# Block-sparse attention and an ELU feed-forward on one core: p and x turned on TensorE as float32, split into two float16 parts out of PSUM

## The chip, the cores and the metric

The kernel runs on one core of a Trainium2 chip. The metric is the device time of one execution, in microseconds (us); lower is better. Engines are named as the profile names them: PE (TensorE), ACT (ScalarE), DVE (VectorE), POOL (GpSimd), and SP, which issues most transfers.

## What is computed

```
scores = q @ k.T / sqrt(64), masked to -1e9 outside the allowed 32x32 blocks   # 4 batches x 8 heads, 768 x 768
attn   = exp(scores - rowmax);  attn = attn / (rowsum + 1e-9)
x      = (attn @ v) laid out as [3072, 512]
h      = x @ w_in                                   # 512 -> 2048
g      = where(h > 0, h, exp(min(h, 0)) - 1)
out    = (g @ w_out) as float32                     # 2048 -> 512
```

A block row may look at its own block and the two beside it, at the first and the last block, and at three sampled ones; the first and last block rows look at everything. q, k and v are float32. The weights arrive with eight bytes per element, and the kernel itself takes them apart.

## The kernel before, in words

Every operand of a matmul is carried as two float16 parts, a high one and a low one (value minus high part), so that products come out nearly as exact as float32. A float32 tile is split by three steps: a cast to float16 (the high part), a subtraction (the low part), and, where the contraction needs the other layout, a turn of both parts.

The 3072 rows of x are worked on in 24 units of 128 rows. `attention(u, t, via)` records one unit: q is loaded, split and turned (`qT`, and `qS` with its halves swapped); the sampled keys are copied side by side into `kG` by POOL; the matching rows of v are fetched into `VT` by SP transfers out of a DRAM copy (`vd`) and by POOL's indirect transfers. Then, for each of four pairs of heads (`hp`): the scores on PE (tile `s`), the row maximum on DVE (`m`), the exponential on ACT (`e`, float32), the cast (`p`, high part), the subtraction (low part), the turn of both parts (`pT`), and the product with v on PE (`av`, or `w` by its bank). DVE adds up the parts into `x` (code name `x32`), and after four pairs it normalises x; x is split and turned likewise (`xn`, then `xT`). `ffn(U, t)` records the feed-forward of two units (256 rows): 16 times two products `h`, the ELU in three steps on ACT and DVE (`fe`), its split (`g`), and the products `o` that add into two PSUM banks. The 32 pieces of the weights are loaded, taken apart and split by `weights` while the first units run; nearly all of this is over when the first feed-forward ends.

A turn goes one of two ways, which `via` says. By DMA (`DMA_TRANSPOSE`), or on PE with `turn16`: eight 128x128 float16 transposes (four of the high part, four of the low one) into one PSUM bank, and one copy of 1024 columns out of it, on ACT or DVE. Units 0 to 3 turn q, p and x on PE; units 4 to 13 turn the first two of their four p on PE and the rest by DMA; from unit 14 on everything goes by DMA. Unit 8, the one of the first and last block rows (`sp`), has three p per pair.

What is recorded is a `Plan`: each operation has the engines that may do it with a cost for each, a due time (`t`), and the buffers that it reads and writes. `Plan.order` walks through these in a model of the five engines and of the transfers, and writes down one fixed order for each engine; where an operation may run on two engines, it takes the one that ends it sooner. So a change of a few operations changes the order, and the choice of engine, of everything behind it. Buffers rotate: there are two of `e`, two of `p`, four of `pT`, two of `s` (a PSUM bank each), one `av` and two `o`.

The low part of p is put on POOL or DVE, whichever is free (`LO`), the cast on ACT or DVE (`CAST`), the copy out of PSUM on ACT or DVE (`LEAVE`).

Of the kernel before, what the change touches and what calls it, by code (L numbers as in the profile page):

```python
# [8 lines left out]
F32 = mybir.dt.float32  # L9
# [4 lines left out]
ALU = mybir.AluOpType  # L14
# [211 lines left out]
def kernel(  # L226
# [56 lines left out]
    def const(shape, dtype, name):  # L283
        return sb.tile(shape, dtype, tag=name, name=name)
# [4 lines left out]
    def flat(ap):  # L289
        names = "abcd"[: len(ap.shape) - 1]  # L290
        return ap.rearrange(f"p {' '.join(names)} -> p ({' '.join(names)})")
# [3 lines left out]
    def scaled(eng, dst, src, scale=1.0):  # L295
        if eng == "ACT":
            nc.scalar.activation(dst, src, AF.Copy, scale=scale)
        elif scale == 1.0:
            ENG[eng].tensor_copy(dst, src)  # L299
        else:  # L300
            ENG[eng].tensor_scalar(dst, src, scale, None, op0=ALU.mult)
# [11 lines left out]
    wo = [wo_all[:, f] for f in range(NFC)]  # L313
    kT = [const([P, H, S], F16, f"kT{x}") for x in range(2)]
    kG = const([P, rooms["kG"], 2, H, KW], F16, "kG")
    ident = sb.tile([P, P], F32, tag="x32", bufs=rooms["x32"], name="ident")
    nc.gpsimd.memset(ident, 1.0)
    nc.gpsimd.affine_select(
        ident, ident, pattern=[[1, P]], compare_op=ALU.is_equal, fill=0.0, base=0,
# [54 lines left out]
    def turn16(t, src, dst, via, new=(), w=(), name="", bank="s"):  # L374
# [12 lines left out]
        def leave(e):  # L387
# [3 lines left out]
        plan.add(LEAVE, t, leave, r=[pt], new=new, w=w,  # L391
                 margin=ML, port=False, name=name)

    LO = {"DVE": 0.66, "POOL": 1.2}
    CAST = {"ACT": 0.57, "DVE": 0.43}
    LEAVE = {"ACT": 0.98, "DVE": 0.64}
# [259 lines left out]
    def attention(u, t, via):  # L656
# [105 lines left out]
        for hp in range(H // 2):  # L762
# [46 lines left out]
            for c in range(NC):  # L809
                e32, p, pT = buf("e", [P, 2, 256], F32), buf("p", [P, 2, 512], F16), buf("g" if u == 1 else "pT", [P, 8, P], F16)  # L810
                pts.append(pT)

                def exp(e, c=c, e32=e32, m=m, ss=ss):
                    for y in range(2):
                        nc.scalar.activation(  # L815
                            e32.ap[:, y, :], ss[c].ap[:, y, :], AF.Exp, bias=m.ap[:, 6 + y : 7 + y])
                plan.add({"ACT": 0.82}, t + PITCH * hp + 1, exp, r=[ss[c], m], new=[e32], name=f"ex{u}.{hp}")
                plan.add(CAST, t + PITCH * hp + 1, margin=MC, fn=lambda e, e32=e32, p=p: scaled(e, p.ap[:, 0, :], flat(e32.ap)),
                         r=[e32], new=[p], name=f"ph{u}.{hp}")
                plan.add(LO, t + PITCH * hp + 1, margin=MO, fn=lambda e, e32=e32, p=p: ENG[e].tensor_tensor(  # L820
                    p.ap[:, 1, :], flat(e32.ap), p.ap[:, 0, :], op=ALU.subtract), r=[e32, p], w=[p],
                    name=f"pl{u}.{hp}")
                turn16(t + PITCH * hp + TURN, p, lambda pT=pT: pT.ap, "PE" if hp < via[1] else "DMA", new=[pT], name=f"pt{u}.{hp}", bank=bank)
# [19 lines left out]
            def join(e, hp=hp, av=av):  # L843
# [3 lines left out]
            plan.add({"DVE": 0.45}, t + PITCH * hp + TIMES + 1, join, r=[av],  # L847
                     new=[x32] if hp == 0 else [], w=[x32] if hp else [], port=False, name=f"nx{u}.{hp}")

        def norm(e):  # L850
            total, x = x32.ap[:, :, D], x32.ap[:, :, 0:D]
            nc.vector.tensor_scalar(total, total, 1e-9, None, op0=ALU.add)
            nc.vector.reciprocal(total, total)
            nc.vector.tensor_tensor(x, x, total.unsqueeze(2).to_broadcast([P, H, D]), op=ALU.mult)
        plan.add({"DVE": 0.95}, t + PITCH * 3 + TIMES + 1.5, norm, r=[x32], w=[x32], name=f"nx{u}")
        U, a = u // 2, u % 2
        if a == 0:
            xT[U] = buf("xT", [P, 2, NCC, 2 * P], F16)
        xt = xT[U]
        ts_ = slice(a * P, (a + 1) * P)  # L860
        new = [xt] if a == 0 else []
        xn = buf("xn", [P, 2, DM], F16)
        plan.add(CAST, t + PITCH * 3 + TIMES + 2, margin=MC, fn=lambda e: scaled(e, by_head(xn.ap[:, 0]), x32.ap[:, :, 0:D]), r=[x32], new=[xn], name=f"xh{u}")
        plan.add(LO, t + PITCH * 3 + TIMES + 2, margin=MO, fn=lambda e: ENG[e].tensor_tensor(
# [119 lines left out]
```

## Time and profile before

| | us |
|---|---|
| runs timed, median of 3 (lowest, highest) | 768.63 (768.42, 770.69) |
| the profiled execution, first to last instruction | 780.8 |
| its PE / DVE / ACT / POOL busy | 703.2 / 504.7 / 406.1 / 398.8 |
| PE's granted clock, mean over the span | 0.934 of full speed |

The profiled execution is one of its own, 12.2 us longer than the median of the timed runs; the profile gives its time as its span. Durations are read from it, and differences worked out in it are carried over to the median. An engine counts as busy while one of its instructions runs; a wait is put down to the instruction that ended it.

### The profile page before, as it was taken

The page shows a single profiled execution, that of the slowest core. Times are in us where ns is not written, and L with a number is a line of the kernel's source. Part 1 is how long each engine was busy: PE and PEld are TensorE (multiplying, and loading weights), DVE is VectorE, ACT ScalarE, POOL GpSimd, SP SyncE. Part 2 cuts the span into 40 slices and gives each one's busy share as a digit, 9 for nine tenths or more (in the row PEclk, how much of TensorE's full clock was granted, in tenths as well). Part 3 has the DMA queues.
Part 4 walks back from the last instruction along what each step waited for, and adds up shares of the span by engine and source line. Part 5 has one row for each costly group of instructions (what it writes and reads, how often), then busy time and mean ns, then how long its engine had stood idle before and what let it go on. Part 6 is the DMA issues. An engine that isn't in the chain of part 4 may idle for free.

```text
span 780.8 us, 26302 instructions
## 1 busy us (share of the span) xinstructions
PE 703.2 (90%) x11064; PEld 476.2 (61%) x11064; DVE 504.7 (65%) x849; ACT 406.1 (52%) x723; POOL 398.8 (51%) x605
## 2 busy tenths in 40 slices
PE   6445466999999998999999999999999999999997
PEld 3334355666665765666866766657656667676663
DVE  7788778898866772767677665757555546644121
ACT  4597767897753743535575443425414344342221
POOL 2588567677553345554375454645625337443121
PEclk7555569999999999999999999999999999999999
DMA  9899998889749697769947987987349459652101
GB/s 240 263 275 288 261 257 209 215 158 208 154 91 264 187 192 164 161 133 203 221 87 142 171 149 150 183 144 166 76 94 229 69 103 216 141 97 45 38 1 27
DMA packets 217006, 126.34 MB, mean 162 GB/s; under 512 B 173944, under 2 KB 194552, under 8 KB 216888
## 3 DMA queue, kind: packets, MB, share of 16 engines
q1 hardware_dynamic: 211608, 107.09, 64.8%
q0 software_dynamic: 5280, 17.58, 8.9%
q8 instruction: 86, 1.41, 0.8%
q14 instruction: 32, 0.26, 0.1%
HBM read 82.05 MB, written 13.21 MB: 122 GB/s over the span
## 4 chain that ended last, share of the span: by engine, by line
PE 80%; issue 4%; DMA 4%; DVE 4%; ACT 3%; POOL 3%; POOLq 1%; SPq 1%; another core or an unknown queue 1%; ACTq 0%; DVEq 0%
PE o L906 32%; PE h L883 31%; PE s L786 6%; PE w L835 4%; PE av L835 2%; PE s L385 2%; DMA wo<-in_moe_w_out_dram 2%; ACT e L815 1%; PE av L385 1%; POOLq L751 1%; DMA VT<-vd 1%; POOL kG L755 1%; DMA raw<-in_sampled_blocks_dram 1%; POOL kG L748 1%
## 5 line engine op out<-in xcount | busy, mean ns | idle before, releaser
L883 PE MATMUL h<-xT,wi 128*128 128x256 f16 x2304 | 281.6, 275 | 4.7 <-DVE fe L891 4.0
L906 PE MATMUL o<-wo,g 128*128 128x512 f16 x1152 | 274.9, 381 | 0.9 <-issue 0.6
L883 PEld LDWEIGHTS <-wi 128*128 128x128 f16 x2304 | 220.0, 98 | 53.8 <-issue 7.1
L906 PEld LDWEIGHTS <-g 128*128 128x128 f16 x1152 | 107.0, 98 | 111.2 <-issue 4.2
L900 POOL TENSOR_TENSOR g<-fe,g 128x512 f16<-128x512 f32 x75 | 90.0, 1200 | 150.8 <-DVE g L299 134.8
L820 POOL TENSOR_TENSOR p<-e,p 128x512 f16<-128x512 f32 x94 | 113.1, 1206 | 93.8 <-DVE p L299 46.4
L893 ACT ACTIVATE fe<-h 128x512 f32<-128x512 f32 x96 | 57.3, 596 | 178.0 <-PE h L883 165.1
L891 DVE SCALAR_TENSOR_TENSOR fe<-h,fe 128x512 f32<-128x512 f32 x96 | 66.0, 688 | 92.9 <-ACT fe L895 84.4
L815 ACT ACTIVATE e<-s,m 128x256 f32<-128x256 f32 x208 | 86.2, 470 | 74.7 <-POOL p L820 37.1
L755 POOL COPY kG<-kT 128x128 int32 x264 | 78.5, 341 | 44.9 <-PE s L786 25.9
L797 DVE TENSOR_REDUCE m<-s 128x2 f32<-128x512 f32 x104 | 70.1, 686 | 44.4 <-PE s L786 41.4
L733 POOL DMA_INDIRECT VT<-vd,idx x66 | 64.5, 977 | 25.1 <-issue 10.1
L895 ACT ACTIVATE fe<-fe,gs 128x512 f32<-128x512 f32 x96 | 69.4, 723 | 2.4
L844 DVE TENSOR_REDUCE x<-w 128x130 f32<-128x260 f32 x64 | 27.2, 426 | 59.7 <-PE w L835 56.9
L835 PEld LDWEIGHTS <-pT 128*32 128x32 f16 x3456 | 43.2, 97 | 36.1 <-issue 33.7
L786 PE MATMUL s<-kG,qT 128*32 128x160 f16 x704 | 44.8, 247 | 9.6 <-ACT e L815 7.0
L786 PEld LDWEIGHTS <-qT 128*32 128x32 f16 x1664 | 33.2, 99 | 31.8 <-issue 26.7
L786 PE MATMUL s<-kT,qT 128*32 128x96 f16 (+1 forms) x832 | 48.5, 225 | 1.2 <-issue 1.0
L786 PE MATMUL s<-kT,qS 128*32 128x96 f16 (+1 forms) x832 | 48.3, 225 | 0.5 <-issue 0.5
L786 PE MATMUL s<-kG,qS 128*32 128x160 f16 x704 | 44.2, 246 | 4.1 <-DVE qS L299 2.7
L299 DVE CAST p<-e 128x512 f16<-128x512 f32 x59 | 32.0, 546 | 13.3 <-DMA pT<-p 6.1
L786 PEld LDWEIGHTS <-qS 128*32 128x32 f16 x1664 | 34.5, 102 | 6.0 <-DVE qS L299 3.0
(134 smaller groups left out, 812.5 us busy)
## 6 DMA issues: line engine op xcount, KB each, us to landing
VT<-vd SPq DMA_DIRECT2D x44, 195.0 KB
VT<-vd SPq DMA_DIRECT2D x22, 390.0 KB
wo<-in_moe_w_out_dram SPq DMA_DIRECT2D x12, 512.0 KB
st<-in_q_dram SPq DMA_DIRECT2D x40, 128.0 KB
out_dram<-ro SPq DMA_DIRECT2D x38, 128.0 KB
wo<-in_moe_w_in_dram SPq DMA_DIRECT2D x9, 512.0 KB
st<-in_moe_w_in_dram SPq DMA_DIRECT2D x7, 512.0 KB
VT<-vd SPq DMA_DIRECT2D x12, 260.0 KB
```

Source lines behind the costliest of these rows:

```text
L733: nc.gpsimd.indirect_dma_start(VT[0:96, 2 * vt.slot, xs[0] : xs[-1] + 1].rearrange("p b x -> p (b x)"), None, d.ap, bass.IndirectOffsetOnA ...
L755: nc.gpsimd.tensor_copy(dst[:, :, r * 16 : (r + 1) * 16], src[:, :, bass.ds(at[r], 16)])
L786: nc.tensor.matmul(dst, lhsT=qq.ap[:, h, j * BLK : (j + 1) * BLK], rhs=mv, start=first, stop=(y == 1 and qq is qS and o0 + w == 256))
L797: nc.vector.tensor_reduce(m.ap[:, 2 * c : 2 * c + 2] if sp else m.ap[:, 6:8], ss[c].ap, axis=AX.X, op=ALU.max, negate=True)
L815: nc.scalar.activation(e32.ap[:, y, :], ss[c].ap[:, y, :], AF.Exp, bias=m.ap[:, 6 + y : 7 + y])
L820: plan.add(LO, t + PITCH * hp + 1, margin=MO, fn=lambda e, e32=e32, p=p: ENG[e].tensor_tensor(p.ap[:, 1, :], flat(e32.ap), p.ap[:, 0, :], ...
L835: nc.tensor.matmul(av.ap[j * BLK : (j + 1) * BLK, y, v0:], lhsT=pts[c].ap[:, pl * 4 + y * 2 + z, j * BLK : (j + 1) * BLK], rhs=VT[:, room, ...
L883: nc.tensor.matmul(h.ap[:, a, :], lhsT=w[:, wl, cs], rhs=x.ap[:, xl, cc, :], start=(n == 0), stop=(n == 3 * NCC - 1))
L891: nc.vector.scalar_tensor_tensor(e32.ap, h.ap, -IH * GS, e32.ap, op0=ALU.mult, op1=ALU.min)
L895: plan.add({"ACT": 0.68}, p0 + 2.6, lambda e, e32=e32: nc.scalar.activation(e32.ap, e32.ap, AF.Relu, bias=gs_col, scale=-GS), r=[e32], w=[ ...
L900: plan.add(LO, p0 + 2.6, margin=MO, fn=lambda e, e32=e32, g=g: ENG[e].tensor_tensor(g.ap[:, 1], e32.ap, g.ap[:, 0], op=ALU.subtract), r=[e ...
L906: nc.tensor.matmul(o.ap, lhsT=g.ap[:, gl, f % 2, m * P : (m + 1) * P], rhs=wo[f][:, wl, :], start=(f == 0 and n == 0), stop=(f == NFC - 1 ...
```

## The change

Where a p or an x is turned on PE (and the unit isn't the special one, for p), the new helper `turn32` takes the place of cast, subtraction and `turn16`: four 128x128 float32 transposes of the float32 tile itself (`e`, or the normalised x) into one PSUM bank, then ACT writes the high part out of PSUM, and DVE writes the low part as PSUM minus high part. The normalised x is written into a float32 tile of its own (`xf`, in the room of `xn`). The identity for these transposes is float32 and now has a room of its own; before it shared the room of x. It concerns 38 turns: 34 of p and 4 of x. What is turned by DMA stays as it was.

```diff
-    ident = sb.tile([P, P], F32, tag="x32", bufs=rooms["x32"], name="ident")
+    ident = const([P, P], F32, "ident")
...
+    def turn32(t, src, part, high, low, new=(), w=(), name="", bank="s"):
+
+        pt = buf(bank, [P, 4, P], F32, ps)
+
+        def go(e):
+            for i in range(4):
+                nc.tensor.transpose(pt.ap[:, i, :], part(i), ident)
+        plan.add({"PE": TURN32}, t, go, r=[src], new=[pt], code=8, name=name + "p")
+        plan.add(HIGH, t, lambda e: scaled(e, high(), pt.ap), r=[pt], new=new, w=w, margin=MC, port=False, name=name)
+        plan.add({"DVE": 0.69}, t, lambda e: nc.vector.tensor_tensor(low(), pt.ap, high(), op=ALU.subtract),
+                 r=[pt, *new, *w], w=[*new, *w], port=False, name=name + "l")
+
+    TURN32, HIGH = 0.6, {"ACT": 0.6}
...
+                if hp < via[1] and not sp:
+                    turn32(t + PITCH * hp + TURN, e32, lambda i, e32=e32: flat(e32.ap)[:, i * P : (i + 1) * P],
+                           lambda pT=pT: pT.ap[:, 0:4], lambda pT=pT: pT.ap[:, 4:8], new=[pT], name=f"pt{u}.{hp}", bank=bank)
+                    continue
...
+        xf = buf("xn", [P, DM], F32) if via[2] == "PE" else None
...
-            nc.vector.tensor_tensor(x, x, total.unsqueeze(2).to_broadcast([P, H, D]), op=ALU.mult)
-        plan.add({"DVE": 0.95}, t + PITCH * 3 + TIMES + 1.5, norm, r=[x32], w=[x32], name=f"nx{u}")
+            nc.vector.tensor_tensor(
+                x if xf is None else by_head(xf.ap), x, total.unsqueeze(2).to_broadcast([P, H, D]), op=ALU.mult)
+        plan.add({"DVE": 0.95}, t + PITCH * 3 + TIMES + 1.5, norm, r=[x32], w=[x32], new=[xf] if xf else [], name=f"nx{u}")
...
+        if via[2] == "PE":
+            turn32(t + PITCH * 3 + TIMES + 3, xf, lambda i: xf.ap[:, i * P : (i + 1) * P],
+                   lambda: xt.ap[:, 0, :, ts_], lambda: xt.ap[:, 1, :, ts_],
+                   new=new, w=[] if new else [xt], name=f"xt{u}", bank="av")
+            return
```

Since the change is a few operations in a plan, it shows best in the orders that come out. In all, PE loses 304 float16 transposes with a weight load each and gets 152 float32 ones; of the subtractions of p, POOL's go from 94 to 62. Three places follow.

PE, at the first turn of a p in the program, before: the last rows of a scores group, then the turn, which goes on like this for eight weight loads and eight matmuls.

```order
L786 LDWEIGHTS qS_621
L786 MATMUL s_757<-kT_70,qS_621 32x96
L385 LDWEIGHTS p_747
L385 MATMUL o_795<-ident_76,p_747 128x128
L385 LDWEIGHTS p_747
L385 MATMUL o_795<-ident_76,p_747 128x128
```

The same place now: the turn is four matmuls that read `e` itself.

```order
L799 LDWEIGHTS qS_621
L799 MATMUL s_660<-kT_70,qS_621 32x96
L400 MATMUL o_713<-ident,e_708 128x128 x4
L799 LDWEIGHTS qT_617
L799 MATMUL s_723<-kG,qT_617 32x160
```

The weight loads of the turn have no rows of their own in the new order, and the turn comes after two pairs of scores, where before four pairs came first.

SP's queue, where v of the second batch goes to DRAM (`vd_183`) and comes back for unit 1 (L726 to L728), before; `wo` and `st` rows are pieces of weights and `in_q_dram` rows are q of the units 2 and 3:

```order
L569 DMA vd_183<-VT 7x16x1040 x2
L569 DMA vd_183<-VT 16x1040 x2
L429 DMA st_1457<-in_moe_w_in_dram 128x4x256
L640 DMA st_1499<-in_q_dram 64x8x64 x2
L640 DMA st_1514<-in_q_dram 64x8x64 x2
L429 DMA wo<-in_moe_w_in_dram 128x4x256
L726 DMA VT<-vd_183 32x1040
L727 DMA VT<-vd_183 32x1040
L728 DMA VT<-vd_183 96x1040
```

And now:

```order
L582 DMA vd_183<-VT 7x16x1040 x2
L582 DMA vd_183<-VT 16x1040 x2
L446 DMA wo<-in_moe_w_out_dram 128x1024 x2
L442 DMA wo<-in_moe_w_in_dram 128x4x256
L442 DMA st_1415<-in_moe_w_in_dram 128x4x256
L739 DMA VT<-vd_183 32x1040
L740 DMA VT<-vd_183 32x1040
L741 DMA VT<-vd_183 96x1040
```

The four loads of q that stood between have moved behind unit 1's v, and over the whole queue 14 pieces of weights stand ahead of that v instead of 16.

ACT, in unit 1 (whose turned p lies in a room of `g`), before: `e` rows are exponentials, `p` the cast, `g` the copy of 1024 columns out of PSUM, `wo`, `wi` and `w` steps of the weights.

```order
L815 ACTIVATE e_1335<-s_1114,m_1166 128x256 x2
L439 ACTIVATE wo<-wo 128x512
L297 ACTIVATE p_1342<-e_1335 128x512
L297 ACTIVATE wi<-wo 128x512
L444 ACTIVATE w_1383<-wo 128x512
L439 ACTIVATE wo<-wo 128x512
L297 ACTIVATE g_1397<-o_1385 128x1024
```

And now, in the same unit:

```order
L828 ACTIVATE e_1107<-s_1026,m_1102 128x256 x2
L828 ACTIVATE e_1111<-s_1062,m_1105 128x256 x2
L297 ACTIVATE g_1152<-o_1114 128x512
L452 ACTIVATE wo<-wo 128x512
L457 ACTIVATE w_1197<-wo 128x512
L297 ACTIVATE g_1235<-o_1155 128x512
```

Cast and wide copy are gone; one copy of 512 columns per pair (the high part) stands in their place, and exponentials follow each other directly. Ahead of the first product `h` of the feed-forward, PE's order had 13 pairs of scores before and has 8 now; both have the same 8 products with v there.

## Rows read from the trace of the kernel before

**Rows 1.** The page: busy time of each engine, and the span in 40 slices.
```profile
PE 703.2 (90%) x11064; PEld 476.2 (61%) x11064; DVE 504.7 (65%) x849; ACT 406.1 (52%) x723; POOL 398.8 (51%) x605
...
PE   6445466999999998999999999999999999999997
...
DVE  7788778898866772767677665757555546644121
...
PEclk7555569999999999999999999999999999999999
DMA  9899998889749697769947987987349459652101
```

**Rows 2.** Busy time by stage: PE, PEld, DVE, ACT, POOL; clock, DMA share, GB/s.
```profile
40.00:113.00 73.00, 38.18 (x793) 29.39 (x792) 59.91 (x88) 58.16 (x102) 52.57 (x87) 0.55 0.96 266
113.00:160.00 47.00, 39.03 (x772) 27.19 (x769) 39.45 (x65) 38.69 (x69) 30.54 (x36) 0.92 0.89 222
160.00:700.00 540.00, 528.47 (x8651) 355.92 (x8649) 354.78 (x600) 266.76 (x492) 279.26 (x411) 1.00 0.78 155
```

**Rows 3.** The chain that ended last, 59 to 76 us: start, us, what.
```profile
59.49 1.12 POOL p L820
60.63 0.84 ACT e L815 x2
...
72.33 1.16 POOL p L820
73.49 0.05 issue
73.53 0.62 PE o L385 x4
74.18 1.02 ACT g L297
```

**Rows 4.** Waits: who waited for whom, us in total, times, longest.
```profile
ACT e L815 <- POOL p L820: 44.9, 28, 4.4
```

**Rows 5.** Groups of instructions by line and shape: busy us, mean ns of one, idle before.
```profile
L299 DVE CAST p<-e 128x512 f16<-128x512 f32 x59 | 32.0, 546 | 13.3 <-DMA pT<-p 6.1 <-ACT e L815 5.0 <-issue 1.0
L297 ACT ACTIVATE p<-e 128x512 f16<-128x512 f32 x53 | 33.4, 629 | 0.9 <-DMA pT<-p 0.4 <-PE av L385 0.2
L820 POOL TENSOR_TENSOR p<-e,p 128x512 f16<-128x512 f32 x94 | 113.1, 1206 | 93.8 <-DVE p L299 46.4 <-ACT p L297 22.4 <-issue 12.4
L297 ACT ACTIVATE pT<-s 128x1024 f16<-128x1024 f16 x15 | 15.3, 1020 | 4.9 <-PE s L385 4.8
L893 ACT ACTIVATE fe<-h 128x512 f32<-128x512 f32 x96 | 57.3, 596 | 178.0 <-PE h L883 165.1 <-POOL xn L864 4.6 <-issue 3.2
L891 DVE SCALAR_TENSOR_TENSOR fe<-h,fe 128x512 f32<-128x512 f32 x96 | 66.0, 688 | 92.9 <-ACT fe L895 84.4 <-POOL kG L755 3.1 <-ACT kT L297 1.8
```

**Rows 6.** The chain at full clock, 154 to 158 us: one turn, one product with v, one scores group.
```profile
154.74 0.45 PE av L385 x8
...
156.93 0.46 PE av L835 x32
157.40 0.54 PE s L786 x32
```

**Rows 7.** Instructions on tile p: ns min, median, max, first and last start.
```profile
L385 PEld LDWEIGHTS <-p x320: 95/98/152, 44.4 to 424.9; 128*128 128x128 f16 x160
```

**Rows 8.** Timeline of SP, 66 to 87 us: start, us, line, transfer.
```profile
66.00 6.49 SPq L569 DMA_DIRECT2D vd<-VT  x4
72.54 0.42 SPq L429 DMA_DIRECT2D st<-in_moe_w_in_dram  x1
73.26 6.13 SPq L640 DMA_DIRECT2D st<-in_q_dram  x4
79.49 0.99 SPq L429 DMA_DIRECT2D wo<-in_moe_w_in_dram  x1
80.53 0.50 SPq L726 DMA_DIRECT2D VT<-vd  x1
```

**Rows 9.** Timeline of PE, 91 to 113 us: unit 1's products, its x, the first h.
```profile
91.89 0.61 PE L385 MATMUL s<-ident,p 128*128 128x128 f16 x4 [1.54 <-ACT p L297]
...
97.30 0.51 PE L835 MATMUL av<-VT,g 128*32 128x130 f16 x12
...
105.69 0.84 PE L835 MATMUL av<-VT,g 128*32 128x130 f16 x32
109.43 0.61 PE L385 MATMUL av<-ident,xn 128*128 128x128 f16 x4 [2.90 <-ACT xn L297]
...
113.00 1.97 PE L883 MATMUL h<-xT,wi 128*128 128x256 f16 x12
```

**Rows 10.** PE on L883 (h) and on L906 (o), up to 160 us.
```profile
0.00:160.00 160.00, 17.21 (x124) 0.69 0.92 250
...
0.00:160.00 160.00, 9.75 (x36) 0.69 0.92 250
```

## Prediction

> **What bounds the kernel now.** I read the page first, for the places where PE is full. It is busy for 90% of the span, but the slices say more: through the seventh (some 137 us) PE is at 4 to 6 tenths, with its clock at 5 to 7 tenths of full speed in the first six, and from the eighth on it is nearly always at 9, with the clock near full speed to the end [rows 1]. The table by stage makes two stages of it [rows 2]. From 160 to 700 us PE works 528.5 of 540 us: there every column that PE is given or spared moves the end, and what happens on ACT, DVE and POOL (49 to 66% busy) costs nothing unless PE waits for it. From 40 to 113 us PE works 38 of 73 us at a granted clock of 0.55, that is, mostly at the lower of its two levels, 1.2 GHz; DVE works 59.9, ACT 58.2, POOL 52.6, and the DMA engines are 96% busy. The first `h` starts at 113.00 [rows 9]. So the start is a matter of the chain that leads to that `h`, and the rest a matter of PE's work.
>
> In the start, the chain of waits runs through the very steps that the change takes out. At 59.49 POOL makes a low part of p, the next exponential follows at once; at 72.33 a low part, then half a turn on PE (0.62 at the low clock), then ACT's wide copy (1.02) [rows 3]. The waits agree: ACT's exponentials waited 44.9 us in all for POOL's low parts, since there are two buffers of `e` and the low part is what frees one [rows 4]; the part of it that lies behind turns by DMA stays.
>
> **The change, part by part.**
>
> *Other engines.* One turn of p cost a cast (0.63 us on ACT, 0.55 on DVE), a low part (1.21 on POOL), and a wide copy (1.02 on ACT) [rows 5]. It now costs ACT a copy of 512 columns out of PSUM and DVE a subtraction that reads PSUM; neither is in the trace, but the nearest rows are ACT's 512 columns out of PSUM at 0.60 and DVE's at 0.69 [rows 5], and I take these. Behind an exponential the path was 0.63 + 1.21 + 0.45 + 1.02 = 3.3 us, with two changes of engine more than now; it becomes the turn + 0.60 + 0.69, about 1.9 us. The exponential's buffer is freed by PE, no longer by POOL.
>
> Counted over what stands in each engine's order ahead of the first step of the first feed-forward, with durations such as these: POOL has 13 low parts of p less (15.7 us), 2 of x (2.4), 4 gathers and 6 key copies (5.9), and one split of weights more: about 23 us less. ACT has 10 half exponentials less (4.7), 9 casts (5.7), 12 wide copies (12.2) and some 2 us of other things, and 10 narrow copies more (6.0): about 19 less. DVE gets 11 subtractions from PSUM (7.6) and loses 7 casts, 3 low parts and 2 copies (about as much); it has only some 7 us less, because work of later units now stands behind that point. DVE, the busiest of the three, thus gains nothing from the change itself. In the PE-bound stage all this is cover: the cost there is nothing, and if PE did wait for it, a turn's 0.69 on DVE is what would show.
>
> *The first `h`.* A lower bound for what it gains is DVE's 7 us. The upper one follows the chain. SP holds the q of units 2 and 3 from 73.26 for 6.13 us, then a piece of weights, and only at 80.53 issues unit 1's v [rows 8]; the q loads now stand behind it, so it can be issued some 7 us sooner. PE works at pairs of unit 2 from 91.89 before unit 1's first product at 97.30 [rows 9]; these are now behind unit 1: up to 5 us. From unit 1's last product to `h` it takes 7.3 us (105.69 to 113.00), with PE waiting 2.90 us for the cast of x [rows 9]; now a join (0.4), the normalisation (1.1), a cold turn (about 1.2), 0.60, 0.69 and five handovers (0.8 in all): 4.8, so 2.5 less. That makes 14 or 15. I take the middle, 11 us: each of these can run into DVE or the DMA engines.
>
> Not all of it is kept. Ahead of the first `h` PE did 13 pairs of scores and now does 8, so 5 pairs come later. A pair is 0.54 (scores) + 0.45 (turn) + 0.46 (product) = 1.45 us at full clock [rows 6]: 7.3 us. From 113 to 160 us PE stood idle for 47.0 - 39.0 = 8.0 us [rows 2], and I let half of the deferred work find room there. What the end gains is 11 - 3.6 = 7.4 us.
>
> *PE's own work.* A turn of eight float16 transposes is 0.45 us at full clock [rows 6], 56 ns for each with its weight load hidden. There is no float32 transpose in this trace. The lower bound is four at the same 56 ns, 0.22 us. The upper one is four passes over the array for each, 0.90, and if each pass also waits for its weight load (98 ns [rows 7]) 16 x 0.154 = 2.46. Between them lies one pass whose weight load isn't hidden: 4 x (0.098 + 0.056) = 0.62. I take 0.62: the order has no separate weight loads for these turns any more that could run ahead, and the bytes to load are those of eight float16 tiles, in half as many pieces, so less than 0.45 would need a faster path. The page "TensorE: Matmul & The Clock Gate" of the Trainium skill (Weight-path perf modes) speaks against the change here: the fast weight load is on only where the type isn't float32, and a plain load of 128 columns is given there as about 107 ns, which as an estimate would make it 4 x (0.107 + 0.056) = 0.65 us, and what PE pays below 4.4 us; no run here shows it, and my sum goes by 0.62.
>
> Which turns pay? By 160 us the trace had done about 10 groups of `h` and 6 of `o` (124 and 36 matmuls, in twelves and sixes) [rows 10], and PE was full. The new order has 16 of the 38 float32 turns ahead of that point, 22 behind. The 16 lie where PE has slack. The 22 cost 22 x (0.62 - 0.45) = 3.7 us.
>
> *What costs nothing.* The identity's own room, the normalised x in another tile (the same instruction of DVE), and PE's shorter list of instructions: nothing that waits today waits for these. The plan orders the whole program anew, which moves single waits of 1 to 3 us either way; I put 2 us of the range down to it.
>
> *The sum.* -7.4 + 3.7 = -3.7 us. Against the profiled execution's 780.8 that is 777.1; taken off the runs' median, 768.6 - 3.7 = 764.9, so 765.
>
> **The rivals.**
>
> *One pass with the load hidden* (0.22 us a turn). For it: in the float16 turns of this trace every load is hidden. Then the 22 turns give 22 x 0.23 = 5.1 back, and the sum is -7.4 - 5.1 = -12.5: 756. The Trainium skill's page "TensorE: Matmul & The Clock Gate" (Terms, the row on the buses) has a transpose mode that is four times faster for float32, which would bring it near this case; this trace can't say.
>
> *Four passes* (0.90 us or more a turn); this one ends on the other side. It acts in the PE-bound stage: 22 x 0.45 = 9.9 us more, with the start's gain +2.5: 771. If each pass waits for its load (2.46), 22 x 2.01 = 44 and the time is 805. It decides from the point at which 22 x (turn - 0.45) eats 7.4 us, a turn of 0.79 us. For it: float32 has twice the bytes of what these rows show. The Trainium skill's page "FP8 and Floating Point Precision" (TensorE Precision Notes) counts four passes for a true float32 product; whether a transpose is one, only the run can tell.
>
> *The start gains nothing.* The change moves a subtraction onto DVE for every turn, and up to 113 us DVE and the DMA engines are the busiest [rows 2]; the pieces of weights ahead of the first step of the feed-forward are as many as before. Against it: the chain names POOL and ACT there, not DVE [rows 3]. If so, only PE's cost is left: +3.7, 772; with four passes as well 778.
>
> **How the numbers follow.** Something under 0.3%, 2.3 us, can't be told from no change. My forecast, faster by about 4 us, has 0.40, of which 0.30 lies beyond that bound, 0.08 within it and 0.02 on the other side. The hidden load has 0.15, all faster. Four passes have 0.20: 0.02 faster, 0.05 within, 0.13 slower. The start without a gain has 0.25: 0.02, 0.10 and 0.13. Together: faster 0.49, same 0.23, slower 0.28. The range runs from the hidden load's 756 to 776, between the start without a gain (772) and that together with four passes (778). For the forecast alone it is 761 to 769.
>
> **What would show it.** In the new profile, the float32 turns are a group of their own: four matmuls on `e`, whose spacing at full clock gives the turn directly, 0.62 if I am right, 0.22 or 0.90 if a rival is. The first `h` should start near 102 us; near 113 the start has gained nothing, near 98 all of it. POOL's low parts of p should number 62, and ACT's wait for them in the first 100 us be gone. From 160 us to the end PE should stay full; new gaps behind DVE's subtractions there would be a cost that I have at nothing. The prediction fails most easily by the turn: above 0.79 us it eats the gain.

## The result, and the profile after

The changed kernel is slower: 777.96 us (median of 4 runs, 775.57 to 782.92) against 769.66 for the kernel before, timed beside it on the same chip; ratio 1.0109, interval 1.0082 to 1.0135. I had forecast 765, with 756 to 776 as the range. The profiled execution of the change has a span of 775.0 us and a time of 776.86. Rows 1 to 10 come from an execution of the kernel before that was unusually long (a span of 780.8); a second profile of it, taken in the first experiment, has a span of 770.4 and a time of 772.11. Where the two kernels are compared below, it is with that one.

The page of the changed kernel, the two lines of busy time that answer to [rows 1], and POOL's low parts, as in [rows 5]:

```profile
PE 695.7 (90%) x10912; PEld 470.0 (61%) x10912; DVE 488.8 (63%) x848; ACT 385.8 (50%) x710; POOL 371.4 (48%) x581
...
PE   6545268999989999998999999999999999999997
...
L837 POOL TENSOR_TENSOR p<-e,p 128x512 f16<-128x512 f32 x62 | 74.3, 1199 | 64.6 <-DVE p L299 27.1
```

Everything that the change names is there: POOL makes 62 low parts instead of 94, and PE, DVE, ACT and POOL all have less to do than in [rows 1]. The wait that the change was to remove fell from 44.9 us [rows 4] to 23.8 (the table of waits):

```profile
ACT e L828 <- POOL p L837: 23.8, 13, 4.4
```

But this total says little of the start. Of the 44.9 us, the trace of before has this up to 140 us, and 42.8 us behind 160:

```profile
ACT e L815 <- POOL p L820: 2.1, 1, 2.1
```

In the changed kernel these 2.1 us are gone. What the low parts held up in the start of before was PE's own turns: 4.9 us of PE's waits up to 140 us end with one (tile o, L385).

The new operations themselves (L400 turns, L403 writes the low part; ns min/median/max, first and last start), and one turn at full clock in the chain of waits:

```profile
L400 PEld LDWEIGHTS av<-ident,e x56: 138/141/230, 209.1 to 414.6; 128*128 128x128 f32 x56
L400 PE MATMUL av<-ident,e x56: 272/273/421, 209.3 to 414.7; 128*128 128x128 f32 x56
...
L403 DVE TENSOR_TENSOR pT<-av,pT x14: 673/682/692, 211.5 to 415.6; 128x512 f16<-128x512 f32 x14
...
225.10 0.44 PE av L400 x4
```

A float32 turn takes PE 0.44 us, as long as the eight float16 transposes did (0.45, [rows 6]). A record of one transpose lasts 273 ns, but the four overlap: what counts is the step of the chain, 110 ns for one.

By stage (as [rows 2]) the changed kernel:

```profile
40.00:113.00 73.00, 33.18 (x632) 24.18 (x633) 53.81 (x87) 46.85 (x86) 36.15 (x63) 0.56 0.94 263
113.00:160.00 47.00, 42.34 (x773) 30.53 (x772) 41.89 (x71) 42.77 (x81) 28.62 (x44) 1.00 0.93 219
160.00:700.00 540.00, 527.96 (x8724) 354.68 (x8722) 347.46 (x601) 257.06 (x487) 273.19 (x407) 1.00 0.82 157
```

and the last stage in the second profile of before:

```profile
160.00:700.00 540.00, 535.22 (x8813) 362.12 (x8802) 363.60 (x611) 272.20 (x502) 285.63 (x416) 1.00 0.83 158
```

From 160 to 700 us PE works 7.3 us less than before in the same time, although DVE, ACT and POOL have less to do. In this stage PE's time is the end's time, so this is where the loss is to be looked for. What PE stood for is in the table of its waits, 113 to 700 us (us in total, times, longest), of the changed kernel:

```profile
PE w L852 <- issue: 2.6, 1, 2.6
PE o L931 <- issue: 2.3, 1, 2.3
PE h L908 <- issue: 2.3, 2, 1.4
```

and of the second profile of before, where this is all of its kind (the first, unusually long one has 7.3; more on it at the end of the account):

```profile
PE o L906 <- issue: 1.0, 1, 1.0
```

"issue" is a wait for nothing that the profile shows: no semaphore, no other engine. 7.2 us against 1.0. One of the four stops in PE's timeline:

```profile
354.26 0.54 PE L852 MATMUL w<-VT,pT 128*32 128x130 f16 x32
...
356.13 0.53 PE L852 MATMUL w<-VT,pT 128*32 128x130 f16 x32
356.60 1.49 PE L908 MATMUL h<-xT,wi 128*128 128x256 f16 x12
358.01 0.53 PE L852 MATMUL w<-VT,pT 128*32 128x130 f16 x30
361.11 0.21 PE L852 MATMUL w<-VT,pT 128*32 128x65 f16 x2 [2.58 <-issue]
```

PE stops in the middle of a product, 30 of 32 matmuls in, with all its operands there. Counted through the trace, the matmul behind each of these four stops is PE's instruction 4546, 5314, 10177 and 15298 (counted from 0, in order of their starts): 193 or 194 modulo 256, every time, and the same four in a second profile of the changed kernel. The trace has 85 transfers of 16 KB in a queue of kind "instruction" for PE's 21872 instructions, one for 256. And each stop ends with a landing: in the two profiles of the changed kernel PE goes on 1.4 to 1.6 us after one of these transfers has landed, eight times of eight. So PE had run out of instructions: the next block of 256 had not come in time. What the DMA engines did meanwhile, the DMA view of 350 to 362 us shows (busy tenths of the DMA engines, queues with packets, MB, share of 16 engines):

```profile
DMA  6999999987999999999999999999998999999999
...
q1 hardware_dynamic: 3410, 2.01, 78.1%
...
q8 instruction: 1, 0.02, 0.6%
```

One block of instructions among 2.8 MB of v and k, with the DMA engines at 90% or more in nearly every slice. PE passed into the block before at 352.6; the packet landed 7.0 us later (it started only after 5.8 us and took 1.2), while the block itself, with three products of v in it (64 instructions in half a microsecond each), ran in 5.7.

A stop can cost twice. Behind the one at 217 us, in this profile, the clock falls to half (columns as above, the clock third from the end):

```profile
213.00:217.00 4.00, 3.90 (x114) 2.92 (x114) 4.00 (x8) 3.23 (x8) 3.56 (x4) 1.00 1.22 149
...
219.60:223.00 3.40, 3.40 (x36) 2.04 (x40) 0.00 (x0) 0.60 (x1) 1.16 (x1) 0.50 0.64 108
```

PE idled 2.3 us and then worked 3.4 us at 1.2 GHz: 1.7 us more. It is one of eight: behind the same stop in the second profile (2.4 us) and behind the longer one at 361 us (2.6) the granted clock stays at 1.00. Why it fell here and not there, no run shows.

### The profile page after: what moved, and what is told of

It is laid out like the page before. It is cut to its first block, busy times and chain, and to the rows that moved or that the text cites. A ratio compares the mean times of both kernels' runs of the same rounds, so it can differ in the third digit from the quotient of the medians.

```text
span 775.0 us, 25974 instructions
## 1 busy us (share of the span) xinstructions
PE 695.7 (90%) x10912; PEld 470.0 (61%) x10912; DVE 488.8 (63%) x848; ACT 385.8 (50%) x710; POOL 371.4 (48%) x581
## 4 chain that ended last, share of the span: by engine, by line
PE 71%; DMA 13%; DVE 6%; issue 3%; ACT 3%; SPq 2%; POOL 2%; POOLq 1%; DVEq 0%; ACTq 0%
PE o L931 30%; PE h L908 28%; PE s L799 5%; PE w L852 4%; DMA wo<-in_moe_w_in_dram 2%; DMA st<-in_moe_w_in_dram 2%; DMA st<-in_q_dram 2%; PE av L852 2%; DMA st<-in_moe_w_out_dram 2%; PE s L385 1%; DMA VT<-vd 1%; DMA pT<-p 1%; DMA wo<-in_k_dram 1%; DMA wo<-in_moe_w_out_dram 1%; DVE w L464 1%
## 5 line engine op out<-in xcount | busy, mean ns | idle before, releaser
L931 PEld LDWEIGHTS <-g 128*128 128x128 f16 x1152 | 106.2, 98 | 112.8 <-issue 4.3
L925 POOL TENSOR_TENSOR g<-fe,g 128x512 f16<-128x512 f32 x80 | 97.1, 1214 | 155.1 <-DVE g L299 135.0
L837 POOL TENSOR_TENSOR p<-e,p 128x512 f16<-128x512 f32 x62 | 74.3, 1199 | 64.6 <-DVE p L299 27.1
L852 PEld LDWEIGHTS <-pT 128*32 128x32 f16 x3456 | 42.8, 97 | 35.8 <-issue 32.1
L299 DVE CAST g<-fe 128x512 f16<-128x512 f32 x71 | 37.1, 523 | 2.3
L889 POOL TENSOR_TENSOR xn<-x,xn 128x512 f16<-128x512 f32 x13 | 15.6, 1200 | 47.2 <-DVE xn L299 24.5
```

The lines of the kernel that those rows point to most:

```text
L852: nc.tensor.matmul(av.ap[j * BLK : (j + 1) * BLK, y, v0:], lhsT=pts[c].ap[:, pl * 4 + y * 2 + z, j * BLK : (j + 1) * BLK], rhs=VT[:, room, ...
L925: plan.add(LO, p0 + 2.6, margin=MO, fn=lambda e, e32=e32, g=g: ENG[e].tensor_tensor(g.ap[:, 1], e32.ap, g.ap[:, 0], op=ALU.subtract), r=[e ...
L931: nc.tensor.matmul(o.ap, lhsT=g.ap[:, gl, f % 2, m * P : (m + 1) * P], rhs=wo[f][:, wl, :], start=(f == 0 and n == 0), stop=(f == NFC - 1 ...
```

## The experiments

Two theories were on record. The theory of the operations, S: the float32 turns, or ACT's and DVE's parts of them, cost the time. The theory of the order: the operations cost nothing, and the new order in which the plan puts everything behind them does; after the first four runs it became theory F, that in the new order PE's blocks of instructions come late. All medians are of runs beside the kernel before on the same chip.

| run | us, median | before | ratio, interval | stops of PE, 113 to 700 us |
|---|---|---|---|---|
| e1_before_again | 770.89 | 769.87 | 1.0011 (0.9990 to 1.0031) | 1.0 |
| e2_after_again | 780.64 | 769.87 | 1.0148 (1.0105 to 1.0191) | 7.2 |
| e3_p_only | 774.53 | 769.87 | 1.0068 (1.0042 to 1.0094) | 5.8 |
| e4_x_only | 775.10 | 769.87 | 1.0047 (1.0016 to 1.0079) | 1.6 |
| f1_after_moved_64 | 771.23 | 769.78 | 1.0013 (0.9994 to 1.0033) | 5.7 |
| f2_before_moved_96 | 772.86 | 769.78 | 1.0032 (1.0014 to 1.0051) | 4.8 |
| f3_turns_in_old_order | 777.97 | 769.78 | 1.0105 (1.0081 to 1.0129) | 1.2 |
| f4_after_turn_at_044 | 772.42 | 769.78 | 1.0040 (1.0025 to 1.0056) | 0 |
| g1_044_moved_128 | 775.83 | 770.49 | 1.0069 (1.0039 to 1.0099) | 3.1 |
| g2_after_right_count | 780.04 | 770.49 | 1.0133 (1.0085 to 1.0181) | 3.7 |
| g3_before_right_count | 773.51 | 770.49 | 1.0038 (1.0017 to 1.0060) | 0 |
| h1_before_few_loads | 767.74 | 769.92 | 0.9963 (0.9946 to 0.9980) | 0.3 |
| h2_after_few_loads | 766.49 | 769.92 | 0.9963 (0.9945 to 0.9981) | 0 |
| h3_right_count_few_loads | 771.23 | 769.92 | 1.0016 (0.9997 to 1.0035) | 0 |
| h4_old_order_few_loads | 774.12 | 769.92 | 1.0077 (1.0048 to 1.0105) | 0 |
| i1_044_moved_32 | 786.49 | 782.92 | 1.0041 (1.0024 to 1.0057) | 5.5, in pieces of up to 0.5 |

The stops are the "issue" rows of PE's table of waits of the one profiled execution. Up to h4, 31 of these 32 stops stand at an instruction 193 or 194 modulo 256 by the count, and 30 of the 31 end 1.2 to 1.7 us after an instruction packet landed (the one of e1: 2.1).

**Both kernels again, no edit.**

> The kernel before, unchanged, for a second profile: the first had a span of 780.8 us while the timed runs lie at 768 to 771. If that execution was an odd one, the new profile has a span near 768 us, and the places where it is shorter than 780.8 are what my prediction took for the kernel's normal course. If profiles are simply longer, it is near 780 again. The ratio to itself should be 1.000 within 0.3%.

> The changed kernel, unchanged, for a second profile and to see how far its runs scatter: 775.6 to 782.9 us in four runs. Expected 776 to 780; stalls that stand in both of its profiles belong to its order, those in one only are chance.

The kernel before agrees with itself (1.0011), and its second profile is an ordinary execution. The loss is there again (780.64, just above what was expected), and the four stops at the same four instructions (194.9, 218.7, 358.6 and 522.5 us). By these two profiles the stops belong to the order.

**p alone, and x alone.** In the first the four x keep their cast, low part and float16 turn, in the second the 34 p do:

```diff
-        xf = buf("xn", [P, DM], F32) if via[2] == "PE" else None
+        xf = None
...
-        if via[2] == "PE":
+        if xf is not None:
```

```diff
-                if hp < via[1] and not sp:
+                if False:
```

> Only the 34 turns of p are float32; x is split and turned as before. Theory of the operations (the new turns or DVE's subtractions cost the 8 us): nearly all of it is here, 776 to 778. Theory of the order (the turns cost nothing, the newly written order of the whole plan does): any value from 765 to 780, not in proportion to the number of turns.

> Only the 4 turns of x are float32, all before 165 us; p as before. Theory of the operations: 4 of 38 turns, so within 1 us of before, 769 to 771. Theory of the order: the plan is written anew here too, so it may lie 3 to 8 us off in either direction.

Neither went as the theory of the operations said. The four turns of x alone bring a loss of 0.47% (5 us by the medians), where it gave at most 1 us. That four turns of 0.44 us with two short steps each behind them don't cost that, and a new order of everything behind them does, is argued here and not shown: e3 has stops as the full change has (5.8 us, at other places), but e4 only 1.6 us of them, which is less than its loss.

**The same order, other blocks.** Small products are added to the warm-up, while PE has nothing else to do; they move every later instruction by 64 places (f1, on the changed kernel) or 96 (f2, on the kernel before, with 80 in the place of 64) and change no order:

```diff
-        for i in range(32):
+        for i in range(64):
...
-                banks[0][cs, 0:96], lhsT=one[:, 0:32], rhs=one[:, 0:96], start=True, stop=True)
+                banks[0][cs, 0:96 if i < 32 else 32], lhsT=one[:, 0:32], rhs=one[:, 0:96 if i < 32 else 32],
+                start=True, stop=True)
```

> The changed kernel with 32 more of the small warm-up products (32 columns each) in front: the order of every engine and all operations stay, but each PE instruction behind them stands 64 places later in the program. Theory F (PE's instructions come late): in the two traces of the changed kernel PE stood 7.2 us for nothing that the profile shows, always at an instruction whose number is 193 or 194 modulo 256. With the 64 places the dense stretches fall elsewhere on these blocks; counted in the trace, the blocks that run in under 6 us lack 11.7 us in sum instead of 19.7. So the stops at 193, 217, 358 and 523 us should go, others may come, again at 193 or 194 modulo 256, and the stops should sum to 1 to 4 us, the time fall to 771 to 775. Theory S (the float32 turns and what they put on ACT and DVE cost it): 777 to 780, as the changed kernel, wherever PE stops.

> The kernel before with 48 more of the small warm-up products in front: same order, every PE instruction 96 places later. Theory F: counted in the trace of before, the blocks of 256 that run in under 6 us lack 18.8 us in sum instead of 12.4, and the two shortest run in 2.1 us instead of 3.7; so new stops of PE of 2 to 6 us in sum should appear at instructions 193 or 194 modulo 256, and the time be 771 to 776. Theory S: 769 to 771, no change, since no operation of the change is in it.

Both times went as theory F said, one each way. The changed kernel, operation for operation the same, falls to 771.23; the kernel before goes from 1.0 to 4.8 us of stops and takes 3 us more. The stops of f1 missed what was expected (1 to 4 us): they fell only from 7.2 to 5.7, and moved. The largest is now at instruction 8898 (194 modulo 256).

```profile
319.28 0.41 PE L853 MATMUL w<-VT,pT 128*32 128x130 f16 x19
322.40 0.32 PE L853 MATMUL w<-VT,pT 128*32 128x130 f16 x12 [2.72 <-issue]
```

So 1.5 us fewer stops go with 6.7 us less in the median. The profiled executions fit better, since there span and stops belong together: the span less the stops is 767.8 and 766.5 us in the two profiles of the changed kernel (766.1 for the first without the 1.7 us of its clock) and 765.0 in f1.

**The turns in the old order.** The 38 turns become float32 without the plan being told; the casts and low parts that fall away leave empty places, and e and p share four buffers in the place of two each.

```diff
         def go(e):
+            if e32 is not None:
+                for i in range(4):
+                    nc.tensor.transpose(pt.ap[:, i, :], flat(e32.ap)[:, i * P : (i + 1) * P], ident)
+                return
...
         def leave(e):
...
+            if e32 is not None:
+                scaled("ACT", to[:, 0:4], pt.ap)
+                nc.vector.tensor_tensor(to[:, 4:8], pt.ap, to[:, 0:4], op=ALU.subtract)
+                return
```

> All 38 float32 turns with their ACT and DVE parts, but in the order of the kernel before, entry for entry (the casts and low parts that fall away leave empty places; e and p share four rooms). Theory F with the order as cause: the operations themselves cost nothing, so 767 to 772, plus what PE's stops at 193 or 194 modulo 256 add, which the trace tells (the program is 8 places shorter behind every turn, so the blocks fall differently). Theory S: 774 to 780, of which no more than 1 to 2 us lies in such stops.

Here theory F missed and theory S (774 to 780) was right: 777.97 with only 1.2 us of stops. PE's waits from 112 to 468 us, the stretch with turns on PE, tell why (f3, then the second profile of before):

```profile
PE h L902 <- DVE fe L910: 5.9, 2, 5.6
PE av L847 <- DVE x L856: 3.1, 3, 2.3
PE s L794 <- ACT e L826: 2.5, 3, 1.6
PE w L847 <- DVE x L856: 1.2, 1, 1.2
PE s L794 <- DVE qS L679: 1.1, 2, 0.8
```

```profile
PE h L883 <- DVE fe L891: 4.1, 1, 4.1
PE av L835 <- DVE x L844: 2.9, 2, 1.7
...
PE s L786 <- ACT e L815: 0.9, 1, 0.9
PE s L786 <- DVE qS L671: 0.7, 1, 0.7
PE s L385 <- POOL p L820: 0.7, 1, 0.7
```

All rows of f3 sum to 16.4 us, those of before to 10.3 (in the expectation for h4 I put the first at 17.5): 6.1 of the 8.2 us that f3 loses. One copy by one engine has become a copy by ACT and then a subtraction by DVE, and the order of before, so I read it, has no place for the second. So the operations aren't free as such. They come near it only in an order made for them.

**Another order of the same operations**, from the measured turn, and that order moved by 128 places as in f1 (g1):

```diff
-    TURN32, HIGH = 0.6, {"ACT": 0.6}
+    TURN32, HIGH = 0.44, {"ACT": 0.6}
```

> The changed kernel with the turn's cost in the plan set to the measured 0.44 us (0.6 before): the same operations in another order. Theory F: where the blocks of instructions fall is thrown anew; 768 to 780, and the time less PE's stops agrees with that of the changed kernel less its 7.2 us to within 2 us. Theory S: 776 to 780, whatever the order, and not tied to the stops.

> The kernel of f4_after_turn_at_044 (772.4 us, no stop of PE in its trace after 113 us) with 64 more small warm-up products in front, so that every PE instruction stands 128 places later: same order, same operations. Theory F: counted in the trace of f4, the blocks of 256 instructions that run in under 6 us then lack 22.1 us in sum instead of 12.1, three of them in about 3 us; so 4 to 9 us of stops at instructions 193 or 194 modulo 256, and 775 to 781 us. Theory S, or an order that is simply better: 770 to 774, unchanged.

f4 has no stop in its trace and 772.42 us, 5.5 less than the changed kernel with the same operations, and within 2 us of that kernel less its 7.2 us of stops, as theory F said. Moved, it stops again (instructions 2241 and 12226, 193 and 194 modulo 256) and takes 775.83: the direction and the low end of the range that theory F gave, with 3.1 us of stops where it gave 4 to 9.

**The plan's count put right.** The plan keeps count of PE's instructions, to keep dense stretches apart, but begins at 0 where PE has already had 112 for its warm-up; the chip's blocks end elsewhere. 196 makes up for it:

```diff
-        code, block = 0, -FETCH_TIME
+        code, block = 196, -FETCH_TIME
```

(g2 on the kernel of f4, g3 on the kernel before.)

> The changed kernel with the turn's cost at 0.44 and with the plan's count of PE instructions begun at 196 instead of 0, so that its blocks end where the chip's do (192 modulo 256 in the program, behind 112 warm-up instructions and some 20 waits). In the plan's own numbers no block then runs in under 5 us (5.4 us lacking in sum for the changed kernel where its blocks really end). Theory F: stops of 0 to 2 us, time 764 to 769, faster than before. Theory S: 774 to 780.

> The kernel before with only the plan's count of PE instructions begun at 196. Theory F: before has only 1 us of stops to lose in its trace, so 766 to 770, at best 1 to 3 us faster, another order all the same; it shows what of g2 is the count and what the change. If it gains as much as g2 (both 764 to 768), the change itself is worth nothing; if it stays at 768 to 770 and g2 gains, the float32 turns are worth 2 to 5 us once the order is free of stops.

Both missed: neither is faster than the kernel that it was made from. g2 still has 3.7 us of stops: here a right count, without a right forecast of when packets land, was not enough. g3 has none and is 0.4% slower all the same, so stops aren't all that an order costs. Its first h is at 111.7 us; f4's was at 107.5.

**Fewer transfers.** The transfers of v from unit 4 on are left out, in the three functions that issue them (two are shown), so that the products there use rows of v that earlier units left and the result is no longer the attention; no engine's order is touched.

```diff
                 def load(e, vt=vt, parts=parts):
...
+                    if u >= 4:
+                        return
...
                 def gather(e, vt=vt, parts=parts):
+                    if u >= 4:
+                        return
```

> The kernel before without the transfers of v from unit 4 on (the products there use rows of v that earlier units left in the rooms), all orders as they are. PE waits for no v after 160 us in the trace, so both theories: 765 to 769; theory F takes away the 1 us of stops and the spread between executions.

> The changed kernel without the transfers of v from unit 4 on. Theory F (instruction blocks queued behind data): the stops at 193, 217, 358 and 523 us go or fall under 1.5 us in sum, the time to 763 to 768, that is 1 to 4 us under the kernel before with the same left out, which is what the earlier start is worth. Theory S: 5 to 9 us above the kernel before with the same left out, 772 to 778. A middle way, dense blocks that come late with few transfers too: stops of 3 to 6 us stay, 769 to 773.

> The kernel of g2_after_right_count (780.0 us) without the transfers of v from unit 4 on. Theory F: its 3.7 us of stops go and the spread over executions (777 to 786) with them: 765 to 770. If it stays at 775 or above with no stops, its order is bad for another reason, its start above all (first h at 111.7 us instead of 107).

> The float32 turns in the old order (778.0 us, 1.2 us of stops) without the transfers of v from unit 4 on. The trace of f3 lays its loss on PE's waits for e, x, fe and xT between 112 and 468 us (17.5 us instead of 10.3), that is on ACT's and DVE's parts that the old order has no place for; if so it stays 6 to 9 us above the kernel before with the same left out: 772 to 777. If it falls to that kernel's time, transfers were behind this loss too.

This is the strongest evidence. The changed kernel loses 11.5 us (777.96 to 766.49), the kernel before 1.9 (769.66 to 767.74); by the ratios, 1.0109 and 1.0148 fall to 0.9963, and before lies at 0.9963 too. With the DMA engines at half load the loss is gone. The change is then 1.2 us ahead by the medians, which can't be told from nothing: the runs of h1 lie at 764.9 to 768.4, those of h2 at 763.4 to 769.5. No stop is left in h2, and the same stretch of its timeline that stood still at 358 us runs through:

```profile
349.05 0.53 PE L858 MATMUL w<-VT,pT 128*32 128x130 f16 x32
349.51 1.48 PE L914 MATMUL h<-xT,wi 128*128 128x256 f16 x12
350.93 0.54 PE L858 MATMUL w<-VT,pT 128*32 128x130 f16 x32
```

By stage, h1 and then h2 (clock, DMA share, GB/s at the end):

```profile
160.00:700.00 540.00, 537.20 (x8795) 362.93 (x8784) 351.51 (x608) 268.24 (x495) 241.60 (x367) 1.00 0.52 92
```

```profile
160.00:700.00 540.00, 538.10 (x8898) 362.02 (x8896) 345.95 (x610) 258.55 (x491) 233.28 (x364) 1.00 0.50 91
```

PE works 538.1 of 540 us instead of 528.0, with the DMA engines at 0.50 instead of 0.82. Counted in the traces from 113 us on, 11 blocks of instructions (8 in the second profile) landed more than 5 us after PE had passed into the block before them in the changed kernel, 4 in the kernel before, and none in h1 and h2. The edit takes away more than late blocks, though: POOL issues less, and PE's other waits from 113 to 700 us fall too, from 9.0 to 4.9 us in the changed kernel. What is common to both kernels cancels in a comparison of the profiled executions: the changed kernel's span falls by 13.4 us (775.0 to 761.6; from the second profile 12.1), that of before by 6.1 (770.4 to 764.3). The difference is 7.3 us (6.0 from the second profile). The stops that go make 6.5 us, and the fall of the clock another 1.7 in the first profile alone: that is the size of it. h3 loses its stops and most of its excess, but stays 4.7 us above h2: its first h is at 112.8 us, h2's at 107.3, so its start can be the rest. h4 stays 6.4 us above h1, as the reading of f3 said: what it loses is on ACT and DVE, not in transfers.

**A version to beat the kernel before**: the order of f4, moved by 32 places.

> The kernel of f4_after_turn_at_044 (772.4 us) with 16 more small warm-up products in front, so that every PE instruction stands 32 places later: same order, same operations. Counted in the trace of f4, the blocks that run in under 6 us then lack 8.7 us instead of 12.1. Theory F: stops of 0 to 1.5 us, 767 to 771, even with the kernel before or up to 3 us faster. If blocks come late by chance of the transfers, whatever their lengths: 771 to 775.

This one ran on a chip where the kernel before takes 782.92 us. Theory F missed: it gave at most 1.5 us of stops and a time no longer than that of before, and the ratio is that of f4, as if the move had done nothing. The trace has 5.5 us of stops of another kind, fifteen of up to 0.5 us and none at 193 or 194; what they are, no run shows. So late blocks aren't the only thing that stops PE by "issue". I have no version that beats the kernel before.

## Why the prediction was wrong, step by step

**PE's turn** (0.62 us, +3.7 in the sum; bounds 0.22 to 2.46). It measured 0.44, that is -0.2 us for the 22 turns instead of +3.7. The idea that the weight load lies open was wrong: records of float32 weight loads last about 140 ns where the float16 ones of p last 98 [rows 7], and a transpose every 110 ns in the chain is less than one such load, so load and pass overlap. The estimate that I gave from "TensorE: Matmul & The Clock Gate" of the Trainium skill, 0.65, falls with it; both rivals on the turn (0.22 and 0.90) fall too.

**The other engines.** ACT's high part at 0.60 and DVE's low part at 0.69 were right (0.60 and 0.68 measured), and so was "no wait of PE for them in the PE-bound stage": in the changed kernel PE's waits for pT from 113 us on sum to 2.3 us, 2.0 of them in one piece. That this cover belongs to the order and not to the operations, f3 and h4 show (8.2 and 6.4 us lost without it).

**The first h** (near 102, 11 us sooner). It came at 106.5 and 108.9 us in the two profiles of the changed kernel, 113.0 and 112.5 in those of before: 3.6 to 6.5 us. One reading behind it was wrong: the 44.9 us of ACT's waits for low parts [rows 4], which "agree" in the prediction, lie nearly all behind the start (2.1 us up to 140 us). The front half of the chain was right. SP issued unit 1's v early and PE's products on it ended some 10 us sooner ([rows 8] and [rows 9]: 80.53, 105.69); SP's and PE's timelines of the changed kernel:

```profile
72.70 0.33 SPq L739 DMA_DIRECT2D VT<-vd  x1
```

```profile
95.26 0.84 PE L852 MATMUL av<-VT,g 128*32 128x130 f16 x32 [1.91 <-DVE x L861]
101.88 1.09 PE L400 MATMUL av<-ident,xn 128*128 128x128 f32 x4 [5.78 <-DVE xn L873]
104.60 1.01 PE L385 MATMUL s<-ident,n 128*128 128x128 f16 x8 [1.63 <-ACT wi L297]
105.54 1.06 PE L693 MATMUL s<-ident,n 128*64 128x128 f16 x16
106.53 1.89 PE L908 MATMUL h<-xT,wi 128*128 128x256 f16 x8
```

The last step failed: from unit 1's last product to h I had 4.8 us, and it took 11.3. DVE, which by my own count gained nothing from the change, was busy with the weights (its timeline):

```profile
96.89 0.69 DVE L475 TENSOR_TENSOR wo<-wo 128x512 f16<-128x512 f32 x1 [1.68 <-ACT wo L297]
97.50 0.69 DVE L464 SCALAR_TENSOR_TENSOR w<-wo,w 128x512 int32<-128x512 int32 x1
98.29 0.69 DVE L468 SCALAR_TENSOR_TENSOR wo<-wo,w 128x512 int32<-128x512 int32 x1
99.01 0.43 DVE L299 CAST wo<-wo 128x512 f16<-128x512 f32 x1
99.35 0.42 DVE L861 TENSOR_REDUCE x<-av 128x130 f32<-128x260 f32 x1
```

The product was there by 96.1; its sum stands behind four steps on the weights, the first of which waits for ACT, until 99.35. And PE has 24 transposes of a q (1.9 us) ahead of h. I had priced the chain's own steps and handovers, not what its engines do in between.

**The deferred work** (half of 7.3 us comes back). It fits in kind: in h1 and h2, nearly without stops, the change is 4.3 us ahead at the first h and 2.7 at the end of the span. But the profiled execution of h2 was the fastest of its eleven, so the 2.7 may be luck in part.

**"What costs nothing: PE's shorter list of instructions"** and **2 us of range for the new order**. This is the step that failed the prediction. I had put the shorter list at nothing because nothing waits for it, and 2 us of range on the order for single waits that move. The order of the instructions and their places in the blocks cost 6.2 us of stops in the profile (7.2 against 1.0), 1.7 for a fall of the clock behind one of them, and by h1 and h2 9.5 us in the medians (11.5 - 1.9); of the profiled spans, 6.0 to 7.3, the stops explain most, but what more the medians hold, I have not located. The Trainium skill has the blocks of 256 in "Runtime: NRT & Kernel Launch" (Instruction fetch mechanics), and says that crossing into one is mostly hidden. The traces agree on the blocks and not on the rest: stops of 0.6 to 2.7 us in the two profiles of the changed kernel, where a dense block met busy DMA engines. I didn't weigh it, though the plan in the code counts PE's instructions against blocks.

So by the medians the +8.3 us divide into -1.2 for what the change does (h2 less h1; -2.7 by their spans) and +9.5 that go with the transfers of v. The first has the sign of my sum at a third of its size, but isn't clear of the noise: that the change gains anything by itself is not shown.

What stays open: stops differ from one execution to the next, and a trace shows one. f4's profiled execution (768.66, no stop) was the fastest of its ten, and what its median execution holds no trace shows. So does the spread: 775.6 to 782.9 for the changed kernel, 763.4 to 769.5 for h2. And the first profile of before has 7.3 us of "issue" between 113 and 700 us, as much as the changed kernel: 3.3 us at one place, ten more of up to 0.5 us as in i1, none at 193 or 194 modulo 256. I don't know what that was. The case for late blocks rests on the other profiles, where place and landing go together, and on h1 and h2.

## What to carry to other kernels

In a program of tens of thousands of instructions on PE, a change of a few operations changes all places in the blocks of instructions. Before pricing a small change there, look for stops by "issue" in PE's waits, count the instruction in front of which each stands, see whether an instruction packet landed just before PE went on, and take the sum of such stops (here up to 7 us of 770) as the noise that any edit may draw from anew; then compare the versions with the instructions moved or the transfers thinned, which separates the edit from its luck. A wait is to be counted in the stage where it is to be saved: the 44.9 us read over the whole span were 2.1 in the start. And a chain's gain is to be priced with what its engines have standing between the chain's own steps.

## What the runs showed of the hardware that I had not expected

Four 128x128 float32 transposes on PE take 0.44 us at full clock, no more than eight float16 ones of the same bytes. In the first profile of the changed kernel PE ran dry of instructions where a block of 256 ran in 4.3 to 6.3 us while the packet of the next, among busy DMA engines, landed 5.4 to 7.0 us after that block was entered; a packet of 16 KB among 2.8 MB held up the engine that bounds the kernel. A landing isn't the end of it: in 30 of 31 such stops PE went on 1.2 to 1.7 us later. And an idle time of 2.3 us was followed by 3.4 us at half clock in one profile, but not at the same place in the other.
